# Sparse attention and a routed expert layer on one core: expert 0 run batch by batch among the next batch's attention, x transposed on TensorE, weights cast by their DMA, masks on VectorE

## The chip, the cores and the metric

One core of one Trainium2 chip. The metric is the device time of one execution in microseconds. Each experiment ran beside the kernel before on one chip, but different experiments ran on different chips, so two experiments are best compared by their ratios to the kernel before. "Span" is the length of the one profiled execution, about 1 to 2 us under the time.

The engines: TensorE (PE in the profile; PEld is its weight load, which overlaps: 788.8 and 389.4 us busy in the kernel before's span of 848.3 us), VectorE (DVE), ScalarE (ACT), GpSimd (POOL), SyncE (SP, which here only issues DMAs).

## The reference, cut to what matters

```python
# attention: q, k, v are (4 batches, 8 heads, 768 positions, 64)
k_sum = k.reshape(B, H, 24, 32, D).max(axis=3)      # 24 blocks of 32 keys
v_sum = v.reshape(B, H, 24, 32, D).mean(axis=3)
scores_l = scale * q @ k^T, kept where |i - j| < 16 # a band
scores_s = scale * q @ k_sum^T + log(32)            # 24 summary keys
a = softmax over both together;  x = a @ [v, v_sum] # -> x (3072, 512)

# routing: P = exp(x @ w_gate), 8 rounds of Sinkhorn: rows, columns, * N/E
# experts: for e in range(8):                       # dense: every row, every expert
#     out += P[:, e:e+1] * (relu(x @ w1[e]) @ w2[e])  # 512 -> 1024 -> 512
```

The routing weight multiplies an expert's result at the very end, so expert 0 can be computed before the routing is known, as soon as rows of x exist. Rows of x exist batch by batch, 768 rows each. Both kernels use this, to a very different degree.

The expert matmuls are the bulk of the work: 8 experts x 6 blocks of 512 rows x 64 matmuls (32 for the hidden layer, 32 for the projection) of 512 columns, 3072 in all.

## The kernel before: the parts that matter

Attention goes by pairs of heads (16 pairs, four to a batch). The mask is a multiplication on GpSimd. Results of a batch collect in `x_sb`; x then gets transposed by a way through DRAM ("the bridge").

```python
E_t = [attn.tile([128, G, EW], BF16, name=f"Et{i}") for i in range(NEB)]
for i in range(NEB):                                  # start-up, a row of memsets
    nc.gpsimd.memset(E_t[i][:, :, 0:EPL], 0.0)
    nc.gpsimd.memset(E_t[i][:, :, EPL + WIN:], 0.0)
    ...
    nc.gpsimd.memset(E_sum[i][:, :], 0.0)
...
def head_mask(i, j):
    nc.gpsimd.tensor_tensor(out=et[...], in0=et[...], in1=band[...], op=ALU.mult)
...
def store_batch(b):
    nc.sync.dma_start(out=x_dram[b * 768:(b + 1) * 768, :]..., in_=x_sb[b % NXB][:])
def xbar_batch(b):
    for g in range(KD):
        nc.sync.dma_start_transpose(out=xT[:, g, b * 768:(b + 1) * 768],
                                    in_=x_dram[b * 768:(b + 1) * 768, g * 128:(g + 1) * 128])
```

Of expert 0 only the hidden layer of its first two 512-row blocks is put among the attention of pairs 7 to 15, in halves of 256 columns (`mm1_drip`):

```python
            if i == 7 and PREFILL >= 1:
                drip += [(0, 0, f) for f in range(2 * KF)]
            if i == 10 and PREFILL >= 2:
                drip += [(0, 1, f) for f in range(2 * KF)]
```

The expert stage: the hidden layer has two PSUM buffers (`fpsum`), the projection four. Weights are loaded as fp32 by SyncE into one staging tile and cast by VectorE or ScalarE.

```python
fpsum = ctx.enter_context(tc.tile_pool(name="fpsum", bufs=2, space=...PSUM))
ypsum = ctx.enter_context(tc.tile_pool(name="ypsum", bufs=4, space=...PSUM))
def mm1(e, n, fpool, eng2):                           # hidden layer
    for f in range(KF):
        hp = fpool.tile([128, 512], FP32, tag="h", name="hps")
        for dk in range(KD):
            nc.tensor.matmul(hp[:], lhsT=w1x[e % 2][...], rhs=xT[:, dk, n * 512:(n + 1) * 512], ...)
        # relu out of PSUM: f even on ScalarE, f odd on VectorE
```

The softmax here doesn't subtract the row's maximum and nothing guards it: scores larger than these inputs give would overflow.

Of the kernel before, what the change touches and what calls it, by code (L numbers as in the profile page):

```python
# [13 lines left out]
AX = mybir.AxisListType  # L14


@with_exitstack
def kernel(
# [20 lines left out]
    NG = N // 512  # L39
    SCALE = 1.0 / float(D) ** 0.5  # L40
    WIN = 192
    LIVE = 158
    EPL = 112
    EW = EPL + WIN + 80
    NPAIR = (B * H) // 2

    PREFILL = 2
# [3 lines left out]
    dram = ctx.enter_context(tc.tile_pool(name="dram", bufs=1, space=bass.MemoryType.DRAM))  # L51
    fpsum = ctx.enter_context(tc.tile_pool(name="fpsum", bufs=2, space=bass.MemoryType.PSUM))
# [4 lines left out]
    band = const.tile([128, WIN], BF16)  # L57
    nc.gpsimd.memset(band, 1.0)
    nc.gpsimd.affine_select(out=band, in_=band, compare_op=ALU.is_ge, fill=0.0,
                            base=-1, pattern=[[1, WIN]], channel_multiplier=-1)  # L60
    nc.gpsimd.affine_select(out=band, in_=band, compare_op=ALU.is_ge, fill=0.0,
                            base=31, pattern=[[-1, WIN]], channel_multiplier=1)

    MBW = 148
    m_big = const.tile([128, MBW], BF16)
    nc.gpsimd.memset(m_big, 1.0)
    nc.gpsimd.affine_select(out=m_big, in_=m_big, compare_op=ALU.is_ge, fill=0.0,
                            base=640, pattern=[[-32, MBW]], channel_multiplier=1)
    nc.gpsimd.affine_select(out=m_big, in_=m_big, compare_op=ALU.is_ge, fill=0.0,
                            base=-609, pattern=[[32, MBW]], channel_multiplier=-1)  # L70

# [16 lines left out]
    wst = [persist.tile([128, 4096], FP32, name=f"wst{i}") for i in range(1)]  # L88
    w1_a = persist.tile([128, KD * F], BF16)
    w2_a = persist.tile([128, KF * DM], BF16)  # L90
    hT_sb = [persist.tile([128, KF, 512], BF16, name=f"hT{i}") for i in range(2)]
    nc.gpsimd.memset(crec_sb, 0.0)

    x_dram = dram.tile([N, DM], BF16, name="x_bridge")

    nc.scalar.dma_start(out=wg_f32[:], in_=moe_w_gate.rearrange("(dk p) e -> p dk e", p=128))
    nc.gpsimd.tensor_copy(out=wg_bf[:], in_=wg_f32[:])

    def load_w1(e, st, part=None):
        src = moe_w1[e].rearrange("(dk p) f -> p dk f", p=128)  # L100
        if part is None:
            nc.sync.dma_start(out=wst[st][:], in_=src)
        else:
            nc.sync.dma_start(out=wst[st][:].rearrange("p (dk f) -> p dk f", dk=KD)[:, part, :],
                              in_=src[:, part, :])

    def load_w2(e, st, part=None):
        src = moe_w2[e].rearrange("(fk p) d -> p fk d", p=128)
        if part is None:
            nc.sync.dma_start(out=wst[st][:], in_=src)  # L110
        else:
            nc.sync.dma_start(out=wst[st][:].rearrange("p (fk d) -> p fk d", fk=KF)[:, 2 * part:2 * part + 2, :],
                              in_=src[:, 2 * part:2 * part + 2, :])

    def cast_w(st, dst, eng):
        if eng is nc.scalar:
            nc.scalar.copy(out=dst[:], in_=wst[st][:])  # L117
        else:
            eng.tensor_copy(out=dst[:], in_=wst[st][:])

    w1x = [w1_a, None]
    w2x = [w2_a, None]
    hfill = [None]

    def mm1(e, n, fpool, eng2):
        for f in range(KF):
            hp = fpool.tile([128, 512], FP32, tag="h", name="hps")
            for dk in range(KD):
                nc.tensor.matmul(  # L129
                    hp[:],  # L130
                    lhsT=w1x[e % 2][:, dk * F + f * 128:dk * F + (f + 1) * 128],
                    rhs=xT[:, dk, n * 512:(n + 1) * 512],
                    start=(dk == 0), stop=(dk == KD - 1))
            if f % 2 == 0:
                nc.scalar.activation(out=hT_sb[n % 2][:, f, :], in_=hp[:],  # L135
                                     func=AF.Relu, bias=0.0, scale=1.0)
            else:
                eng2.tensor_scalar_max(out=hT_sb[n % 2][:, f, :], in0=hp[:],  # L138
                                       scalar1=0.0)

    def mm1_drip(e, n, fpool, f):
        hp = hfill[0]
        if f % 2 == 0:
            hp = fpool.tile([128, 512], FP32, tag="h", name="hps")
            hfill[0] = hp
        half = f % 2
        fr = f // 2
        for dk in range(KD):
            nc.tensor.matmul(  # L149
                hp[:, half * 256:half * 256 + 256],  # L150
                lhsT=w1x[e % 2][:, dk * F + fr * 128:dk * F + (fr + 1) * 128],
                rhs=xT[:, dk, n * 512 + half * 256:n * 512 + half * 256 + 256],
                start=(dk == 0), stop=(dk == KD - 1))
        if half == 0:
            nc.scalar.activation(out=hT_sb[n % 2][:, fr, 0:256], in_=hp[:, 0:256],
                                 func=AF.Relu, bias=0.0, scale=1.0)
        else:
            nc.vector.tensor_scalar_max(out=hT_sb[n % 2][:, fr, 256:512],  # L158
                                        in0=hp[:, 256:512], scalar1=0.0)

    with tc.tile_pool(name="attn", bufs=1) as attn, \
         tc.tile_pool(name="pw", bufs=1, space=bass.MemoryType.PSUM) as pw, \
         tc.tile_pool(name="avp", bufs=1, space=bass.MemoryType.PSUM) as avp:

        NQKB = 2
        NVB = 2
        NTRB = 3
        NEB = 4
        NVE = 3
        NXB = 2  # L170

        qq_st = [attn.tile([128, G, 128], FP32, name=f"qqst{i}") for i in range(NQKB)]
        kk_st = [attn.tile([128, G, 128], FP32, name=f"kkst{i}") for i in range(NQKB)]
        vv_f32 = [attn.tile([128, G, 2, 65], FP32, name=f"vvf{i}") for i in range(NVB)]
        qq_bf = [attn.tile([128, G, 128], BF16, name=f"qqb{i}") for i in range(2)]
        kk_bf = [attn.tile([128, G, 128], BF16, name=f"kkb{i}") for i in range(2)]
        vv_ext = [attn.tile([128, G, 2, 65], BF16, name=f"vve{i}") for i in range(NVE)]
        qqT = [attn.tile([128, 16 + S + 48], BF16, name=f"qqT{i}") for i in range(NTRB)]
        kkT = [attn.tile([128, S], BF16, name=f"kkT{i}") for i in range(NTRB)]
        ksumT = [attn.tile([128, 128], BF16, name=f"ksumT{i}") for i in range(NTRB)]  # L180
        E_t = [attn.tile([128, G, EW], BF16, name=f"Et{i}") for i in range(NEB)]
        E_sum = [attn.tile([128, S], BF16, name=f"Esum{i}") for i in range(NEB)]
        vsum_ext = [attn.tile([128, 65], BF16, name=f"vsum{i}") for i in range(NEB)]
        recip = [attn.tile([128, G, 1], FP32, name=f"recip{i}") for i in range(NEB)]
        x_sb = [attn.tile([128, G, DM], BF16, name=f"xsb{i}") for i in range(NXB)]

        for i in range(NVB):
            nc.gpsimd.memset(vv_f32[i][:, :, :, 64:65], 1.0)
        for i in range(NTRB):
            nc.gpsimd.memset(qqT[i][:, 0:16], 0.0)  # L190
            nc.gpsimd.memset(qqT[i][:, 16 + S:], 0.0)
            nc.gpsimd.memset(ksumT[i][:, 24:128], 0.0)
        for i in range(NEB):
            nc.gpsimd.memset(E_t[i][:, :, 0:EPL], 0.0)
            nc.gpsimd.memset(E_t[i][:, :, EPL + WIN:], 0.0)
            nc.gpsimd.memset(E_t[i][:, :, EPL:EPL + 1], 0.0)
            nc.gpsimd.memset(E_t[i][:, :, EPL + 1 + LIVE:EPL + WIN], 0.0)
            nc.gpsimd.memset(E_sum[i][:, :], 0.0)
            nc.gpsimd.memset(vsum_ext[i][:, :], 0.0)
            nc.gpsimd.memset(vsum_ext[i][0:24, 64:65], 32.0)  # L200

        def ptile(shape, dtype, tag, name):
            return pw.tile(shape, dtype, tag="work", name=name, bufs=5)

        def load_pair(i, eng=None, split=False):
            b = i // 4
            h0 = (i % 4) * 2
            eng = eng or nc.sync
            eng2 = nc.scalar if split else eng
            for j in range(2):  # L210
                eng.dma_start(
                    out=qq_st[i % NQKB][:, :, j * 64:(j + 1) * 64],
                    in_=q[b, h0 + j].rearrange("(g p) d -> p g d", p=128))
                eng2.dma_start(
                    out=kk_st[i % NQKB][:, :, j * 64:(j + 1) * 64],
                    in_=k[b, h0 + j].rearrange("(g p) d -> p g d", p=128))
            for j in range(2):
# [130 lines left out]
        for i in range(NPAIR):  # L348
# [3 lines left out]
            if i + 2 < NPAIR:  # L352
                load_pair(i + 2)
# [178 lines left out]
```

## Time and profile before

| | before |
|---|---|
| time, median of 3 runs | 845.96 us (841.19 to 850.69) |
| span of the profiled run | 848.3 us |
| first TensorE instruction of attention | 14.12 us |
| last values matmul of attention | 176.7 us |
| x of the last batch is all back (its routing matmuls wait for the last piece) | 187.5 us |
| one hidden layer of 512 rows, 32 matmuls | 7.14 to 7.15 us |
| one projection of 512 rows, 32 matmuls | 6.91 us |

The page's row of TensorE's busy tenths and of its granted clock, each digit a fortieth of the span (21 us):

```profile
PE   2886787689999999999999999999999999999998
...
PEclk9955599579999999999999999999999999999999
```

The first eight or nine slices are attention: TensorE is partly idle, and the throttle grants it half its clock in a good part of them. After that it is over 90% busy at full clock. This trace has whole stretches of 20 us at 0.50 (80 to 100 us) and at 1.00 (200 us and later), and some with a mean between; what makes the throttle grant one or the other is not shown. A busy digit at half clock is worth half of one at full clock: the 22 values matmuls of a head take 0.68 us at full clock and 1.38 us at half.

The same stage by stretches of 20 us (columns: stretch and length, then busy time and instructions of PE, PEld, DVE, ACT, POOL, then the clock, the DMA share and GB/s):

```profile
80.00:100.00 20.00, 14.69 (x141) 10.34 (x139) 10.30 (x14) 10.16 (x30) 10.27 (x4) 0.50 0.70 170
...
160.00:180.00 20.00, 13.27 (x157) 9.85 (x159) 6.76 (x16) 4.70 (x14) 4.10 (x3) 0.50 0.12 43
```

No engine is full here. The start of the trace (columns: start, duration, engine, line, operation, output and input; in brackets the idle time before it and what ended it):

```profile
5.29 0.66 POOL L194 MEMSET Et_134<- 128x672 bf16 x1
5.48 8.58 DVE L226 CAST qqb_118<-qqst_112 128x768 bf16<-128x768 f32 x1 [4.13 <-DMA qqst_112<-in_q_dram]
...
13.46 0.19 POOL L199 MEMSET vsum_145<- 128x65 bf16 x1
13.98 0.54 DVE L227 CAST kkb_120<-kkst_114 128x768 bf16<-128x768 f32 x1
14.12 0.82 PE L235 MATMUL tq<-ident,qqb_118 128*128 128x128 bf16 x6 [14.12 <-DVE qqb_118 L226]
```

The cast of q takes 8.58 us and the cast of k, of the same shape, 0.54 us. The first one starts inside GpSimd's row of memsets and ends 0.4 us after that row (13.65 us).

The end of attention in the chain of waits (start, duration, what):

```profile
177.60 3.68 DMA x_bridge<-xsb_151
...
181.30 1.14 SPq L327
...
182.49 1.27 SPq L327
...
183.82 3.63 DMA xT<-x_bridge
```

That is the bridge: 10 us from the last x to its transposed copy. The timeline of TensorE in the same 10 us:

```profile
178.46 7.35 PE L451 MATMUL yps<-w_a,hT_97 128*128 128x512 bf16 x27 [0.22 <-issue]
...
185.67 0.81 PE L451 MATMUL yps<-w_a,hT_97 128*128 128x512 bf16 x3
```

These are projections of expert 0 for blocks whose hidden layer had been done inside attention. And the expert stage in the chain of waits:

```profile
401.27 5.35 PE hps L129 x24
...
406.65 0.70 DVE hT_98 L138
...
407.39 1.02 PE hps L129 x4
408.42 6.91 PE yps L451 x32
```

A hidden layer lasts 7.15 us (401.27 to 408.42), the projection with the same number of matmuls 6.91 us. In the hidden layer the chain runs through a 0.70 us eviction on VectorE: the last group had to wait for a PSUM buffer.

### The profile page before, as it was taken

The numbers are of one execution on the slowest core, as the hardware profiler recorded it, in microseconds if no ns is written. First come the engines' busy times: TensorE is split into PE (matmuls) and PEld (weight loads), VectorE is DVE, ScalarE is ACT, GpSimd is POOL, SyncE is SP. The second block draws the span as 40 slices with busy tenths as digits, with TensorE's granted clock in tenths as the row PEclk, the third lists the DMA queues.
The fourth block names the chain that finished last, engine by engine and source line by source line (L and its number), as shares of the span: only waits on it lengthen the run. The fifth ranks groups of instructions, "written<-read, shape, count | busy, mean of one in ns | idle before, by whom it ended". The sixth has DMA issues, their size and how long they took to land.

```text
span 848.3 us, 11203 instructions
## 1 busy us (share of the span) xinstructions
PE 788.8 (93%) x4546; PEld 389.4 (46%) x4608; DVE 402.4 (47%) x623; ACT 221.1 (26%) x434; POOL 77.8 (9%) x85
## 2 busy tenths in 40 slices
PE   2886787689999999999999999999999999999998
PEld 2665565544444444444444444444444444444443
DVE  6754576447655444444454444444544544444443
ACT  2644356523131212221311113113111131111110
POOL 6542334210000000000000000000000000000000
PEclk9955599579999999999999999999999999999999
DMA  9978688544022003200320022002200200001122
GB/s 177 174 179 197 159 186 190 159 114 160 1 100 100 0 1 100 100 1 0 100 100 1 0 100 100 1 0 100 100 1 0 100 1 1 0 1 50 51 99 100
DMA packets 107876, 65.76 MB, mean 78 GB/s; under 512 B 89392, under 2 KB 92464, under 8 KB 107824
## 3 DMA queue, kind: packets, MB, share of 16 engines
q1 hardware_dynamic: 104944, 64.43, 27.3%
q10 hardware_dynamic: 2880, 0.61, 0.5%
q8 instruction: 36, 0.59, 0.3%
q14 instruction: 16, 0.13, 0.1%
HBM read 52.45 MB, written 9.44 MB: 73 GB/s over the span
## 4 chain that ended last, share of the span: by engine, by line
PE 85%; DVE 6%; ACT 3%; issue 2%; DMA 2%; POOL 0%; SPq 0%; ACTq 0%; DVEq 0%; POOLq 0%
PE hps L129 37%; PE yps L451 37%; PE av L310 4%; PE hps L149 2%; PE ss L266 2%; PE sg L255 1%; PE tq L235 1%; PE tk L237 1%; DMA vvf_116<-in_v_dram 1%; PE vs L288 1%; DVE kkb_120 L227 1%; DVE xsb_151 L314 1%; POOL Et_134 L278 0%; DVE ksumT_131 L242 0%; DMA x_bridge<-xsb_151 0%
## 5 line engine op out<-in xcount | busy, mean ns | idle before, releaser
L462 DVE SCALAR_TENSOR_TENSOR out_acc<-yps,P_sb,out_acc 128x512 f32<-128x512 f32 x168 | 125.8, 751 | 153.5 <-PE yps L451 148.0
L129 PE MATMUL hps<-xT,w_b 128*128 128x512 bf16 x753 | 174.8, 378 | 1.6 <-ACT hT_97 L135 0.4
L129 PE MATMUL hps<-xT,w_a 128*128 128x512 bf16 x689 | 161.6, 378 | 1.2 <-DVE hT_98 L138 0.2
L135 ACT ACTIVATE hT_97<-hps 128x512 bf16<-128x512 f32 x92 | 54.9, 597 | 255.4 <-PE hps L129 243.5
L129 PEld LDWEIGHTS <-w_b 128*128 128x128 bf16 x768 | 74.4, 97 | 97.5 <-issue 17.7
L451 PEld LDWEIGHTS <-hT_97 128*128 128x128 bf16 x768 | 75.2, 99 | 91.6 <-issue 2.4
L135 ACT ACTIVATE hT_98<-hps 128x512 bf16<-128x512 f32 x92 | 54.6, 597 | 240.1 <-PE hps L129 232.0
L451 PEld LDWEIGHTS <-hT_98 128*128 128x128 bf16 x768 | 74.9, 98 | 89.1
L138 DVE TENSOR_SCALAR hT_97<-hps 128x512 bf16<-128x512 f32 x92 | 63.6, 692 | 95.7 <-PE hps L129 95.7
L138 DVE TENSOR_SCALAR hT_98<-hps 128x512 bf16<-128x512 f32 x92 | 63.6, 691 | 95.3 <-PE hps L129 95.3
L129 PEld LDWEIGHTS <-w_a 128*128 128x128 bf16 x704 | 67.8, 97 | 88.4 <-issue 16.4
L451 PE MATMUL yps<-w_a,hT_97 128*128 128x512 bf16 x376 | 87.6, 384 | 1.5 <-DVE xsb_151 L314 0.9
L451 PE MATMUL yps<-w_a,hT_98 128*128 128x512 bf16 x376 | 85.2, 379 | 0.5 <-issue 0.2
L451 PE MATMUL yps<-w_b,hT_97 128*128 128x512 bf16 x375 | 84.5, 379 | 0.4
L451 PE MATMUL yps<-w_b,hT_98 128*128 128x512 bf16 x377 | 84.5, 379 | 0.4
L149 PE MATMUL hps<-xT,w_a 128*128 128x256 bf16 x128 | 21.4, 297 | 0.5 <-DVE hT_98 L158 0.5
L278 POOL TENSOR_TENSOR Et_134<-Et_134,band 128x948 bf16<-128x948 bf16 x8 | 17.9, 2240 | 35.3 <-ACT Et_134 L260 35.3
L117 ACT CAST w_b<-wst_94 128x4096 bf16<-128x4096 f32 x4 | 14.4, 3605 | 25.3 <-PE yps L451 21.6
L278 POOL TENSOR_TENSOR Et_136<-Et_136,band 128x948 bf16<-128x948 bf16 x8 | 15.9, 1984 | 50.1 <-ACT Et_136 L260 50.1
L226 DVE CAST qqb_118<-qqst_112 128x768 bf16<-128x768 f32 x8 | 17.5, 2181 | 4.1 <-DMA qqst_112<-in_q_dram 4.1
L235 PE MATMUL tq<-ident,qqb_118 128*128 128x128 bf16 x48 | 5.8, 275 | 14.1 <-DVE qqb_118 L226 14.1
L278 POOL TENSOR_TENSOR Et_137<-Et_137,band 128x948 bf16<-128x948 bf16 x8 | 16.3, 2040 | 6.0 <-ACT Et_137 L260 5.9
(181 smaller groups left out, 575.3 us busy)
## 6 DMA issues: line engine op xcount, KB each, us to landing
wst_94<-in_moe_w_dram SPq DMA_DIRECT2D x14, 2048.0 KB, 8.2
out_dram<-out_acc SPq DMA_DIRECT2D x24, 256.0 KB, 2.0
wst_94<-in_moe_w_dram SPq DMA_DIRECT2D x8, 512.0 KB, 5.2
qqst_112<-in_q_dram SPq DMA_DIRECT2D x16, 192.0 KB, 3.6
qqst_113<-in_q_dram SPq DMA_DIRECT2D x16, 192.0 KB, 3.9
kkst_115<-in_k_dram SPq DMA_DIRECT2D x16, 192.0 KB, 4.1
vvf_117<-in_v_dram SPq DMA_DIRECT2D x16, 192.0 KB, 4.3
vvf_116<-in_v_dram SPq DMA_DIRECT2D x15, 192.0 KB, 4.1
```

The source lines that it names most:

```text
L117: nc.scalar.copy(out=dst[:], in_=wst[st][:])
L129: nc.tensor.matmul(hp[:], lhsT=w1x[e % 2][:, dk * F + f * 128:dk * F + (f + 1) * 128], rhs=xT[:, dk, n * 512:(n + 1) * 512], start=(dk == ...
L135: nc.scalar.activation(out=hT_sb[n % 2][:, f, :], in_=hp[:], func=AF.Relu, bias=0.0, scale=1.0)
L138: eng2.tensor_scalar_max(out=hT_sb[n % 2][:, f, :], in0=hp[:], scalar1=0.0)
L149: nc.tensor.matmul(hp[:, half * 256:half * 256 + 256], lhsT=w1x[e % 2][:, dk * F + fr * 128:dk * F + (fr + 1) * 128], rhs=xT[:, dk, n * 51 ...
L226: nc.vector.tensor_copy(out=qq_bf[i % 2][:], in_=qq_st[i % NQKB][:])
L235: nc.tensor.transpose(tqv[:, g, :], qq_bf[i % 2][:, g, :], ident)
L266: nc.tensor.matmul(ss[:, :], lhsT=ksumT[i % NTRB][p0:p0 + 64, :], rhs=qtile[p0:p0 + 64, 16 + half * 384:16 + (half + 1) * 384], start=True ...
L278: nc.gpsimd.tensor_tensor(out=et[:, :, EPL + 1:EPL + 1 + LIVE], in0=et[:, :, EPL + 1:EPL + 1 + LIVE], in1=band[:, None, 1:1 + LIVE].to_bro ...
L310: nc.tensor.matmul(av[:, c, :], lhsT=lhsT, rhs=rhs, start=(mi == 0), stop=(mi == len(mms) - 1))
L451: nc.tensor.matmul(yp[:], lhsT=hT_sb[n % 2][:, f, t4 * 128:(t4 + 1) * 128], rhs=w2x[e % 2][:, f * DM:(f + 1) * DM], start=(f == 0), stop=( ...
L462: nc.vector.scalar_tensor_tensor(out=out_acc[:, t, :], in0=yp[:], scalar=psl, in1=out_acc[:, t, :], op0=ALU.mult, op1=ALU.add)
```

## The change

The intent: fill TensorE's idle time in attention with expert 0, all of it, batch by batch; drop the bridge; drop the staging casts; give the hidden layer more PSUM buffers. The core of the diff (the rest renames, or packs scores and summary values of two heads into fewer instructions):

```diff
-def head_mask(i, j):
-    nc.gpsimd.tensor_tensor(out=et[...], in0=et[...], in1=band[...], op=ALU.mult)
+    nc.vector.tensor_tensor(out=et, in0=et, in1=band[...], op=ALU.mult)   # in scores(i)

-def store_batch(b): ...      # x to DRAM
-def xbar_batch(b): ...       # transposing load back
+def to_xT(i, xs):            # one pair's x, 6 transposes on TensorE
+    tx = aps.tile([128, S], BF16, tag="a", name="tx")
+    for g in range(G):
+        nc.tensor.transpose(tx[:, g * 128:(g + 1) * 128], xs[:, g, :, :]..., ident)
+    nc.scalar.copy(out=xT[:, dk, b * S:(b + 1) * S], in_=tx[:])

-def load_w1/load_w2 (fp32 by SyncE into staging), cast_w (VectorE or ScalarE)
+def load_w(e, gate=None):    # the DMA casts fp32 to bf16
+    if gate is not None:     # a one-element write makes the load wait for `gate`
+        nc.gpsimd.tensor_copy(out=w1[0:1, 0, 0:1], in_=gate)
+        nc.gpsimd.tensor_copy(out=w2[0:1, 0, 0:1], in_=gate)
+    nc.gpsimd.dma_start(out=w1[:], in_=moe_w1[e]...)
+    nc.gpsimd.dma_start(out=w2[:], in_=moe_w2[e]...)

+for i in range(NP):          # 16 pairs
+    load(i + 2)
+    if i == 1: load_w(0, kst[3][0:1, 0, 0, 0:1])
+    scores(i);  drip(2)
+    transposed(i + 1);  drip(1)
+    vsum(i)
+    if i > 0:
+        to_xT(i - 1, xs)
+        if i % 4 == 0:       # a batch is complete
+            logits(b)
+            fill += first_expert(two halves of 384 rows)   # 8 hidden + 3 projection each
+            if b == 0: load_w(1)
+    drip(1);  xs = values(i);  drip(2)
...
-fpsum 2 buffers for the hidden layer, ypsum 4 for the projection
+mps2 4 buffers for the hidden layer, mps 3 for the projection
```

The last batch of expert 0 runs after attention, with Sinkhorn's steps strewn in between.

## The prediction

> **What bounds it now.** Two stages. Attention lasts until about 177 us, then comes a bubble until 187 us: the chain of waits shows 177.6 to 187.5 us going to the store of x to DRAM and the transposing load back. From 187 us the experts run, and by the busy time per 100 us TensorE is then 99% busy at clock 1.0. The page's "PE 85% of the chain" is mostly this stage.
>
> In attention TensorE isn't the limit. At full clock the 22 values matmuls of a head take 0.68 us, in the half-clock stretches (40 to 100 and 140 to 180 us) 1.39 us. I estimate 3.7 us of TensorE work per head pair, while a pair takes about 10 us: it waits on the chain score, exp (ACT), mask (GpSimd, 1.98 us a head), values.
>
> In the expert stage an (expert, 512 tokens) step takes 14.06 us. The projection's 32 matmuls take 6.91 us (216 ns each[...]); the hidden layer's take 7.15 us. With two PSUM buffers the next group waits for an eviction (0.69 us on DVE plus its latencies, against 0.86 us of matmuls).
>
> **What the change does.**
> 1. Three of four batches of expert 0 (hidden and projection, about 62 us of TensorE) move into attention's idle TensorE time, where before only 64 matmuls' worth were. TensorE per pair becomes 3.7 + 5.6 = 9.3 us. DVE per pair: casts 1.65,[...] reduce 0.95, qT 0.66, x scaling 1.5, sums 0.4, plus 1.6 of expert evictions: about 8.5 us. So pairs 4 to 15 run at about 10.3 us, nearly today's pace, but with expert 0 inside.
> 2. The bridge disappears: about 10 us.
> 3. Four and three PSUM buffers remove the hidden layer's stall: 0.24 us x 42 = 10 us.
> 4. Weights are cast by the DMA: 28.8 us of ACT and 18 us of DVE casts vanish, all off the critical path.
>
> **A loss.** The instruction order shows six hidden matmuls of expert 0 hoisted into pair 3's scores. TensorE runs in order, so it stops there (about 37 us) until w1 of expert 0 lands. GpSimd's queue waits for pair 3's k (about 25 us) and then issues expert 1's w1 *before* expert 0's: 4 MB must pass, sharing the engines with the q, k, v loads (about 200 GB/s in all in the DMA row). I expect it at 50 to 65 us: a stall of about 18 us.
>
> **Sum.** First matmul 13 us; pairs 0 to 2 at 7.5 us, 36 us; stall to 55; rest of pair 3 and pair 4, 69; eleven pairs, 182; leftover 187; last batch's expert 0 (21 us) with sinkhorn and logits, 211; 2688 matmuls at 216 ns = 581, 792; start-up slips, half-clock pairs, tail: about 802.
>
> **Right or wrong.** The chain should have no x bridge; the hidden layer's 32 matmuls take 6.91 us; TensorE is over 90% busy from pair 4 on at clock 1.0; one gap before a w1 matmul at 37 to 55 us; expert 1 starts about 210 us; pairs with filler take 10 to 11 us.
>
> **What would make it wrong.** Casting DMAs much slower than 200 GB/s (longer stall, over 830). DVE bounding the filled pairs at 12 to 13 us (+25 us): masks or casts dearer than estimated. Sinkhorn's DVE chain, now squeezed into 21 us of matmuls, stopping TensorE by over 5 us. Or a smaller stall (785).
>
> Predicted 802 us, range 778 to 828; faster by over 2%: 0.91, within 2%: 0.07, slower: 0.02.

The six other terms of VectorE are estimates from the kernel before's trace (such as 0.55 us for each of three casts, 0.95 us for the reduce, 0.42 to 0.69 us for an expert's eviction) and come to 6.8 us; the author's "about 8.5 us" holds the cut one, too. The pace of 10.3 us a pair was set above TensorE's 9.3 us. The 3.7 us in that is the author's estimate, and rests on the 0.68 us of a head's values and on the timeline of the kernel before at full clock (108 to 125 us, clock 1.00). "TensorE runs in order" was said without a trace; the changed kernel's shows it (under "The stall" below).

## The result, and the profile after

| | before | after |
|---|---|---|
| time, median of 4 runs each | 844.48 us (841.19 to 850.69) | 778.03 us (777.42 to 778.59) |
| ratio | | 0.9208 (95%: 0.917 to 0.9247) |
| span | 848.3 us | 776.6 us |
| first TensorE instruction of attention | 14.12 us | 5.39 us |
| last values matmul | 176.7 us | 160.7 us |
| x of the last batch is all back (in the new kernel, its first routing matmul) | 187.5 us | 166.1 us |
| hidden layer, 32 matmuls of 512 columns | 7.14 to 7.15 us | 6.91 us |
| expert 1 starts | | 191.5 us |

A ratio is the mean time of one kernel's runs over the mean of the other's runs of the same rounds, so it isn't quite the ratio of the medians beside it.

The change is 8% faster. All outputs are right. The time lies at the very edge of the predicted range, 24 us under the central value of 802 us.

The page's rows of TensorE:

```profile
PE   5649999999999999999999999999999999999997
...
PEclk9769999999999999999999999999999999999999
```

Besides the last slice, only the first three are left in which TensorE isn't full. By stretches of 20 us, with the columns as before:

```profile
40.00:60.00 20.00, 10.81 (x140) 8.43 (x141) 10.84 (x26) 5.41 (x9) 0.00 (x0) 0.66 1.05 214
80.00:100.00 20.00, 19.89 (x266) 12.62 (x266) 17.28 (x42) 11.54 (x23) 0.00 (x0) 1.00 0.79 179
140.00:160.00 20.00, 19.71 (x256) 12.93 (x255) 14.03 (x33) 10.70 (x21) 0.00 (x0) 1.00 0.01 2
```

From 60 us to 160 us the stage is bounded by TensorE itself, at full clock, with VectorE at 14 to 18 of 20 us. The one bad stretch is 20 to 60 us, where the DMA share is full (1.05 to 1.14) and the mean clock 0.66 to 0.75. The start, in the timeline:

```profile
4.74 0.60 DVE L199 CAST kb<-kst 128x768 bf16<-128x768 f32 x1 [0.68 <-DMA kst<-in_k_dram]
5.39 0.82 PE L203 MATMUL tk<-ident,kb 128*128 128x128 bf16 x6 [5.39 <-DVE kb L199]
6.37 1.03 POOL L174 MEMSET E_115<- 128x678 bf16 x1
7.61 0.80 DVE L193 CAST vx_121<-vst 128x768 bf16<-128x768 f32 x1 [0.85 <-DMA vst<-in_v_dram]
```

The cast takes 0.60 us in place of 8.58 us: in the new program GpSimd has other work first (mask constants), so its long memsets start at 6.37 us, after the casts of k and q have started (4.74 and 6.12 us). Here it is memsets that stretch: three of the eight take 1.03 to 1.08 us, the others 0.66 to 0.71. The stretch between attention and the last batch, where the bridge was, in TensorE's timeline:

```profile
160.77 3.40 PE L128 MATMUL yps<-w_322,h 128*128 128x512 bf16 x15
...
166.07 0.74 PE L347 MATMUL sink<-wg_bf,xT 128*128 128x8 bf16 x24
166.67 2.60 PE L116 MATMUL hps<-xT,w_321 128*128 128x384 bf16 x15
```

Left-over projections of the batch before cover the last transposes. The expert stage in the chain of waits:

```profile
406.37 4.96 PE hps L116 x23
...
411.38 1.89 PE hps L116 x8
413.27 6.91 PE yps L128 x32
```

No eviction is on the chain any more; the hidden layer takes 6.91 us, too (406.37 to 413.27, rounded in the lines). And the bad stretch. TensorE and VectorE in the timeline, then SyncE's queue, then GpSimd's issue of weights:

```profile
44.81 0.56 DVE L199 CAST kb<-kst 128x768 bf16<-128x768 f32 x1 [8.12 <-DMA kst<-in_k_dram]
45.43 0.82 PE L203 MATMUL tk<-ident,kb 128*128 128x128 bf16 x6 [7.68 <-DVE kb L199]
49.57 0.82 PE L207 MATMUL tq<-ident,qb 128*128 128x128 bf16 x6 [2.04 <-DVE qb L200]
```

```profile
14.42 1.30 SPq L187 DMA_DIRECT2D kst<-in_k_dram  x2
...
20.11 8.50 SPq L187 DMA_DIRECT2D kst<-in_k_dram  x2
28.65 10.64 SPq L187 DMA_DIRECT2D qst<-in_q_dram  x2
39.39 7.63 SPq L191 DMA_DIRECT2D vst<-in_v_dram  x2
```

```profile
18.21 0.89 POOL L109 DMA_DIRECT2D w_810<-in_moe_w_dram  x1
19.10 0.75 POOL L109 DMA_DIRECT2D w_321<-in_moe_w_dram  x1
...
20.71 1.05 POOL L110 DMA_DIRECT2D w_811<-in_moe_w_dram  x1
```

All four weight loads (w1 and w2 of experts 0 and 1, 2 MB of fp32 each) are issued within 3 us, expert 1's w1 (`w_810`) first. From then on an issue of two loads of pair 4's k takes SyncE 8.50 us in place of 1.30 us. TensorE stands still for 7.68 us for pair 4's k, not for weights: expert 0's w1 (`w_321`) took 15.4 us from issue to landing, so it was there at 34.5 us, before its first matmul at 36.4 us.

An account of the 71.7 us between the two spans, cut at the same event in both, the return of the last batch's x. A full-speed expert matmul of 512 columns is 6.91 us / 32 = 0.216 us:

| | before | after | gain |
|---|---|---|---|
| until the first TensorE instruction | 14.1 | 5.4 | 8.7 |
| from there to the return of the last batch's x, less the expert matmuls inside at full speed | 150.3 | 98.5 | 51.8 |
| from there to the end, less the expert matmuls at full speed | 20.5 | 9.3 | 11.2 |

(Before: 187.5 - 14.1 = 173.4 us hold 128 matmuls of 256 columns and 43 of 512, worth 23.1 us. After: 166.1 - 5.4 = 160.7 us hold 192 of 384 columns and 144 of 512, worth 62.2 us. All 3072 together are worth 663.4 us.)

The account sets one execution against one, and that of the kernel before is from the slow end of its times: the medians differ by 66.4 us, not 71.7. Its attention scatters most. In the run with a third PSUM buffer below, which has the same attention code, the last values matmul ends at 168 us and not 176.7. So up to 9 us of the 51.8 us may be scatter.

### The profile page after: what moved, and what is told of

The parts are those of the page before. It is cut to its first block, busy times and chain, and to the rows that moved or that the text cites. A ratio compares the mean times of both kernels' runs of the same rounds, so it can differ in the third digit from the quotient of the medians. Undisturbed runs are those within 1.5% of the kernel's fastest.

```text
span 776.6 us, 10681 instructions
## 1 busy us (share of the span) xinstructions
PE 739.9 (95%) x4545; PEld 368.4 (47%) x4608; DVE 389.8 (50%) x703; ACT 185.3 (24%) x326; POOL 25.5 (3%) x50
## 4 chain that ended last, share of the span: by engine, by line
PE 88%; DVE 4%; SPq 3%; DMA 2%; ACT 1%; issue 1%; ACTq 0%; DVEq 0%
PE yps L128 41%; PE hps L116 40%; PE av L272 3%; SPq L187 2%; DMA qst<-in_q_dram 2%; PE sg L223 1%; PE tq L207 1%; PE vs L249 1%; PE tx L284 0%; DMA vst<-in_v_dram 0%; SPq L191 0%; PE ss L232 0%; DVE ksT_113 L211 0%; DVE h L123 0%; DVE csum_sb L359 0%
## 5 line engine op out<-in xcount | busy, mean ns | idle before, releaser
L128 PEld LDWEIGHTS <-h 128*128 128x128 bf16 x1536 | 149.2, 98 | 177.8 <-DVE h L123 0.3
L120 ACT ACTIVATE h<-hps 128x512 bf16<-128x512 f32 (+1 forms) x200 | 116.2, 581 | 488.0 <-PE hps L116 479.8
L123 DVE TENSOR_SCALAR h<-hps 128x512 bf16<-128x512 f32 (+1 forms) x200 | 133.7, 669 | 164.7 <-PE hps L116 163.1
L116 PE MATMUL hps<-xT,w_321 128*128 128x384 bf16 x256 | 50.8, 330 | 0.0
L128 PE MATMUL yps<-w_322,h 128*128 128x512 bf16 x183 | 43.3, 379 | 0.5 <-issue 0.2
L116 PE MATMUL hps<-xT,w_810 128*128 128x512 bf16 x188 | 42.4, 379 | 0.2
L116 PE MATMUL hps<-xT,w_3081 128*128 128x512 bf16 x189 | 42.3, 379 | 0.2
L128 PE MATMUL yps<-w_4182,h 128*128 128x512 bf16 x189 | 42.3, 379 | 0.2
L116 PE MATMUL hps<-xT,w_5257 128*128 128x512 bf16 x188 | 42.2, 379 | 0.3
L116 PE MATMUL hps<-xT,w_4719 128*128 128x512 bf16 x189 | 42.3, 379 | 0.2
L128 PE MATMUL yps<-w_4720,h 128*128 128x512 bf16 x188 | 42.2, 379 | 0.2
L116 PE MATMUL hps<-xT,w_5795 128*128 128x512 bf16 x188 | 42.2, 379 | 0.2
L128 PE MATMUL yps<-w_3082,h 128*128 128x512 bf16 x188 | 42.2, 379 | 0.2
L128 PE MATMUL yps<-w_3644,h 128*128 128x512 bf16 x188 | 42.2, 379 | 0.2
L116 PE MATMUL hps<-xT,w_3643 128*128 128x512 bf16 x187 | 42.2, 379 | 0.3
L128 PE MATMUL yps<-w_5796,h 128*128 128x512 bf16 x189 | 42.1, 379 | 0.2
L116 PE MATMUL hps<-xT,w_4181 128*128 128x512 bf16 x188 | 42.0, 379 | 0.2
L128 PE MATMUL yps<-w_811,h 128*128 128x512 bf16 x188 | 42.0, 379 | 0.2
L128 PE MATMUL yps<-w_5258,h 128*128 128x512 bf16 x187 | 42.0, 379 | 0.2
L116 PEld LDWEIGHTS <-w_5795 128*128 128x128 bf16 x192 | 18.8, 98 | 22.6
L116 PEld LDWEIGHTS <-w_3643 128*128 128x128 bf16 x192 | 18.8, 98 | 22.6
## 6 DMA issues: line engine op xcount, KB each, us to landing
w_321<-in_moe_w_dram POOLq DMA_DIRECT2D x1, 1024.0 KB, 15.4
```

The lines of the kernel that those rows point to most:

```text
L116: nc.tensor.matmul(hp[:, 0:n], lhsT=w1s[e][:, dk, f * 128:(f + 1) * 128], rhs=xT[:, dk, t0:t0 + n], start=(dk == 0), stop=(dk == KD - 1))
L120: nc.scalar.activation(out=h[:, f, 0:n], in_=hp[:, 0:n], func=AF.Relu, bias=0.0, scale=1.0)
L123: nc.vector.tensor_scalar_max(out=h[:, f, 0:n], in0=hp[:, 0:n], scalar1=0.0)
L128: nc.tensor.matmul(yp[:], lhsT=h[:, f, c * 128:(c + 1) * 128], rhs=w2s[e][:, f, :], start=(f == 0), stop=(f == KF - 1))
```

## The experiments

The theory, formed on the two traces: (A) most of the gain is expert 0 in idle TensorE time; the hidden layer's third and fourth PSUM buffers are worth about 10 us; the early start is worth 6 to 9 us, and it comes from the casts no longer lying beside GpSimd's memsets; masks and weight casts are worth nothing by themselves; and the gap at 40 us comes from the weight queue starving the q, k, v loads. The rivals are named run by run.

### No expert work inside attention

The changed kernel with expert 0 run whole after attention.

```diff
                     logits(b)
-                    for half in range(2):
-                        fill += list(first_expert(b * S + half * HS, HS, mps))
 ...
-b = B - 1
-for half in range(2): for step in first_expert(b * S + half * HS, HS, mps2): ...
+for b in range(B):
+    for half in range(2): for step in first_expert(b * S + half * HS, HS, mps2): ...
```

> The new kernel, but expert 0 of all four batches runs after attention instead of among it. Theory A (the interleave is the main gain: 62 us of expert 0 run in time in which TensorE would otherwise idle): attention without filler keeps the 8.0 us per pair that pairs 1 and 2 show, so it ends about 140 to 147 us instead of 161, and 62 us of experts come after it: about 815 us, +38 over the new kernel's 778. Rival B (attention itself became that much faster, and the filler only stretches it): at most +15, below 793.

Measured: 819.32 us (815.77 to 820.41), ratio to before 0.9675. That is 41 us above the changed kernel. The last values matmul ends at 140 us in place of 160.7 us, and the last batch's x is all back at 142.5 us in place of 166.1 us. So 62 us of expert matmuls before it cost 23.6 us there; the other 39 us ran in time that is idle without them. Theory A holds for the filler. These 39 us are the filler's worth against no filler at all; the kernel before hid a part of its own 23.1 us already.

### The old attention alone, first try

```diff
-    PREFILL = 2
+    PREFILL = 0
```

> The kernel before without its 64 matmuls' worth of expert 0 among attention, to set attention alone beside attention alone (141 us until the last values matmul in the new kernel without filler, 177 us here with its small filler). Theory (the old attention is bound by its own chain of score, exp, mask, values and not by TensorE): attention ends at 172 to 178 us all the same, and the 14 us of matmuls come after it: 855 to 862. Rival (the small filler was what stretched it): attention ends at 160 us or less and the time stays at 844 to 848.

Measured: 850.21 us (847.09 to 852.95), ratio 1.0041 (0.9991 to 1.0092): no difference can be told. The run doesn't answer its question. In its trace 64 hidden matmuls of expert 0 (72 by their weight loads, as some records are missing) still run between 92 and 140 us: they were moved there from the expert stage, as it seems by the scheduler, which found w1 and x ready. A source edit that stops asking for work does not keep a scheduler from doing it; a dependence does.

### The old attention alone, by a dependence

Here the cast of expert 0's w1 first reads a value of the last pair's x, so no hidden matmul can come earlier.

```diff
-    PREFILL = 2
+    PREFILL = 0
-            if i == 7:
-                cast_w(0, w1_a, nc.vector)
         ...
         xbar_batch(B - 1)
+        nc.vector.tensor_copy(out=w1_a[0:1, 0:1], in_=x_sb[(B - 1) % NXB][0:1, G - 1, DM - 1:DM])
+        cast_w(0, w1_a, nc.vector)
     # load and cast of w2 of expert 0 after attention, too
```

> The kernel before with nothing of expert 0 inside attention, this time by data: the cast of expert 0's w1 reads a value of the last pair's x first, so no hidden matmul can be hoisted (the earlier try without filler failed for that). Read: when the last values matmul ends. What the question is: how much of the gain of the attention stage is the new attention itself, and how much is better use of its idle TensorE time. Theory M (most of the 36 us between the two attention stages is filler used better): the old attention alone ends at 150 to 160 us, 10 to 20 us over the new attention alone (141 us). Rival N (the old chain score, exp, mask on GpSimd, values sets the pace, filler or not): it still ends at 168 us or later, and the new attention alone is over 27 us shorter. The whole time is expected at 850 to 875 us (w2 of expert 0 is loaded and cast later too), and no verdict rests on it.

Measured: 862.64 us (861.72 to 866.38), ratio 1.0222. The last values matmuls of this run, and then those of the new attention alone (the run without filler above), in TensorE's timeline:

```profile
169.65 0.25 PE L310 MATMUL av<-vsum,Esum 128*128 128x65 bf16 x1
169.71 0.30 PE L310 MATMUL av<-vve,Et 128*128 128x65 bf16 x2
173.39 10.97 PE L129 MATMUL hps<-xT,w_a 128*128 128x512 bf16 x39 [3.39 <-DVE w_a L119]
```

```profile
139.84 0.19 PE L272 MATMUL av<-vsx,Es 128*128 128x65 bf16 x1
139.87 0.23 PE L272 MATMUL av<-vx,E 128*128 128x65 bf16 x2
```

The old attention alone ends at 170 us. What I expected of theory M, 150 to 160 us, is refuted, and rival N's numbers hold: the old attention is slow without filler, too. From the first TensorE instruction (14.4 and 5.4 us) it lasts 155.6 us, the new one 134.7 us. So of the 51.8 us in the account, about 21 us are a shorter attention, by one execution each. The other 31 us hold three things that these runs don't separate: more of expert 0 in idle time, a shorter way from the last values to the return of x (10.8 us before, 2.4 us in the run without filler), and the scatter named above. So the filler need not be most of the gain over the kernel before, as theory A has it. Which part of the rewritten attention (masks, fewer and larger instructions for scores and summary values, the transposes) makes the 21 us was not taken apart. Nor was the clock: its mean is 0.66 in these 155.6 us and 0.81 in the 134.7 us, so a part of the 21 us may be TensorE's speed and not the shape of the code.

### Two PSUM buffers for the hidden layer in the changed kernel

```diff
-    mps2 = ...(name="mps2", bufs=4, space=PSUM)
+    mps2 = ...(name="mps2", bufs=2, space=PSUM)
```

> The new kernel with two PSUM buffers for the hidden layer after attention instead of four. Theory (the second bank's eviction held TensorE 0.24 us in each step of 64 matmuls): 32 hidden matmuls take 7.15 us again, 42 steps, +10 us: 788. Rival (the steady stage got faster for another cause, as the weight casts that are gone): no change, 778.

Measured: 791.06 us (790.01 to 791.64), ratio 0.9347: 13 us slower than with four. A hidden layer takes 7.20 us in its chain of waits, the projection stays at 6.91 us; 42 hidden layers in experts 1 to 7 make 42 x 0.29 = 12 us.

```profile
411.89 7.20 PE hps L116 x32
```

### A third PSUM buffer in the kernel before

```diff
+            hpool = xpool[0] if f % 3 == 2 else fpool
-            hp = fpool.tile([128, 512], FP32, tag="h", name="hps")
+            hp = hpool.tile([128, 512], FP32, tag="h", name="hps")
-    ypsum bufs=4
+    ypsum bufs=3, and a pool of one buffer as xpool[0]
```

> The kernel before, with a third PSUM bank for the hidden layer after attention (and three instead of four for the projection). Theory: the same stall as in the run with two banks, seen from the other side: 32 hidden matmuls take 6.91 us instead of 7.15, 46 such groups, about -11 us: 834. Rival (in the kernel before something else, such as the weight casts on ACT and VectorE, holds the steady stage): less than -3 us.

Measured: 836.89 us (828.82 to 839.33), ratio 0.9868 (0.9801 to 0.9936): 9 us faster by the medians, which is under the 2% that count as faster but clear of the noise (5 to 17 us by the interval). Its hidden layers take 6.91 us. From both sides the buffers are worth 9 to 13 us. One buffer more is enough.

### GpSimd's memsets on VectorE in the kernel before

```diff
-            nc.gpsimd.memset(E_t[i][:, :, 0:EPL], 0.0)      # and the three others of E_t
-            nc.gpsimd.memset(E_sum[i][:, :], 0.0)
+            nc.vector.memset(E_t[i][:, :, 0:EPL], 0.0)
+            nc.vector.memset(E_sum[i][:, :], 0.0)
```

> The kernel before with the zeroing of its eight attention buffers on VectorE, which idles until 5 us, instead of GpSimd. Theory (the first q cast took 8.58 us on VectorE because GpSimd's row of memsets kept it out): that cast takes 0.6 us, the first matmul starts at 6 to 7 us instead of 14.1, and attention and all that follows moves up by 6 to 8 us: about 838. Rival (the first cast waited for data): the first matmul starts within 1.5 us of before and the time stays within 2 us.

Measured: 840.27 us (836.17 to 840.94), ratio 0.9911 (0.9854 to 0.9969): 6 us faster by the medians, again under 2% but clear of the noise.

```profile
10.86 0.82 PE L235 MATMUL tq<-ident,qqb 128*128 128x128 bf16 x6 [10.86 <-DVE qqb L226]
```

The first matmul comes at 10.86 us in place of 14.12, and no cast at the start takes over 0.57 us (it would have come earlier still, had the scheduler not put the v cast first, which waited for its load until 9.77 us). So the 8.58 us was the memsets beside the cast. The expected first matmul at 6 to 7 us is missed. The start-up's 3.3 us lie within the gain's interval, 3 to 12 us; whether they count to the end in full is not shown.

### Expert 1's weights later

```diff
                 if i == 1:
                     load_w(0, kst[3][0:1, 0, 0, 0:1])
+                if i == 6:
+                    load_w(1, kst[8][0:1, 0, 0, 0:1])
 ...
-                    if b == 0:
-                        load_w(1)
```

> The new kernel, but expert 1's weights are loaded only after pair 8's k has landed, so that 4 MB less run against the q, k, v loads between 18 and 48 us. Theory C (TensorE's gap of 37.7 to 45.4 us is the k of pair 4, starved by the weight queue): the gap shrinks by about the 14 us that those 4 MB take, TensorE's other waits take some back: 766 to 770. Rival D (the gap is the wait for expert 0's w1, as I predicted): w1 of expert 0 comes first in its queue now and lands 8 us earlier, but pair 4's k is as late as before only if it was never the cause; then the gap would end at the landing of w1 and not at that of k. Rival E (the attention stage is bound elsewhere and later pairs give it back): 776 to 779.

Measured: 770.09 us (768.54 to 770.36), ratio 0.9096: 8 us faster than the changed kernel. Pair 4's k transposes in its timeline, to be read against the 45.43 us line above:

```profile
35.97 0.51 PE L203 MATMUL tk<-ident,kb 128*128 128x128 bf16 x6 [0.68 <-DVE kb L199]
```

The wait falls from 7.68 to 0.68 us. Nothing but 4 MB of expert 1's loads was moved, so the gap came with them.

### Every early weight load gated by itself

```diff
-                if i == 1:
-                    load_w(0, kst[3][0:1, 0, 0, 0:1])
+                # w1 of expert 0 waits for kst[3], its w2 for kst[5],
+                # w1 and w2 of expert 1 for kst[15]
-                    if b == 0:
-                        load_w(1)
```

> The new kernel with all early weight loads spread behind the q, k, v loads: w1 of expert 0 after pair 3's k, its w2 after pair 5's, expert 1 after pair 15's. With the run that moved expert 1 alone (770 us) the same theory: every 2 MB that run against the q, k, v loads cost TensorE waits. Expected: the wait of 2.6 us at 31 us and those at 65 to 80 us of that run go, 762 to 766. Rival (the pairs without filler are bound by their own chain at 8 us, and weights no longer matter): 769 to 770, as the earlier run.

Measured: 769.15 us (768.54 to 769.24), ratio 0.9068. The expected 762 to 766 us is missed; it is no better than the simpler gate. A likely reason stands in its timeline, and the next run tests it:

```profile
6.70 0.67 POOL L180 MEMSET E<- 128x678 bf16 x1
7.19 4.83 DVE L199 CAST vx<-vst 128x768 bf16<-128x768 f32 x1 [0.79 <-DMA vst<-in_v_dram]
...
12.62 0.58 PE L229 MATMUL sg<-qT,kT 64*128 64x158 bf16 x6 [5.34 <-DVE vsx L183]
```

The cast of v took 4.83 us beside GpSimd's memsets, where the changed kernel had got away with 0.80 us, and the first scores came at 12.62 us in place of 9.01 us. The instructions stand in the same order in both. What the traces show to differ is under half a microsecond: v's cast starts at 7.19 us in place of 7.61, the memsets at 6.70 in place of 6.37. That this decides it was not tested.

### The same, with the memsets on VectorE: the fastest kernel

```diff
         for t in E_t:
-            nc.gpsimd.memset(t[:, :, 0:EPL], 0.0)
-            nc.gpsimd.memset(t[:, :, EPL + LIVE:], 0.0)
+            nc.vector.memset(t[:, :, 0:EPL], 0.0)
+            nc.vector.memset(t[:, :, EPL + LIVE:], 0.0)
```

> The changed kernel with the weight loads gated one by one as in the last such run (769.2 us), and the memsets of the E buffers on VectorE in place of GpSimd. In that run the first v cast took 4.83 us beside GpSimd's row of memsets, and the first scores came 3.6 us later than in the changed kernel. Theory: with no long memsets on GpSimd the first v cast takes under 1 us, the first scores come at about 9 us, and the time is 765 to 766 us. Rival: the start is not on the path to the end (the loads' queue sets the pace of pairs 0 to 3 whenever they start), and it stays at 768.5 to 770 us.

Measured: 764.91 us (763.85 to 767.21), ratio 0.9055 (0.9004 to 0.9106), about as the theory had it. In its timeline:

```profile
7.84 0.54 DVE L199 CAST vx<-vst 128x768 bf16<-128x768 f32 x1
9.70 0.58 PE L229 MATMUL sg<-qT,kT 64*128 64x158 bf16 x6 [0.74 <-DVE vsx L183]
```

The v cast takes 0.54 us, the first scores come 2.9 us earlier than in the run above, and the median falls by 4.2 us. The size of that is open: the runs are from different chips, the ratios overlap, and the two profiled executions differ by 2.0 us. The memsets, 0.62 us each on VectorE, cost a little in turn: the first k cast waits behind them until 6.90 us. This version beats both kernels, by 13 us the changed one, and there the intervals of the ratios don't overlap.

### The bridge back, for the last batch alone

```diff
+        if i // PB == B - 1: xs = x_sb[:, :, i % PB, :, :]   # collect the last batch's x
-        to_xT(NP - 1, xs)
+        bridge(B - 1)         # store to DRAM, four transposing loads back
```

> The new kernel, but the last batch's x goes to DRAM and comes back through the transposing load as before, instead of TensorE transposes. Prediction on record: the bridge is worth about 10 us. Theory: store 3.7 us, transposing load about 6 us, of which the 5 us of filler left at that point hide about half: +5 to +7 us, 783 to 785; TensorE then has a gap of 5 to 6 us before the logits of the last batch. Rival (TensorE idles for the whole bridge): +10 us.

Measured: 782.29 us (780.86 to 783.32), ratio 0.9239 (0.9198 to 0.928): 4.3 us slower by the medians, though the interval overlaps that of the changed kernel. TensorE waits 2.84 us and then 0.35 us for the transposing loads; left-over projections cover the rest. The v cast at this run's start was held up, too (4.60 us), but its last values matmul ended at 159.1 us, no later than the changed kernel's. So what the trace shows of the bridge is 3.2 us of waits. The prediction had put it at about 10 us.

### Masks on GpSimd in the changed kernel

```diff
-                    nc.vector.tensor_tensor(out=et, in0=et,
+                    nc.gpsimd.tensor_tensor(out=et, in0=et,
```

> The new kernel with the four masks of a pair back on GpSimd. Theory (the filled pairs are bound by TensorE at 9.0 us, the mask is hidden by filler matmuls; only pairs 0 to 3 see the longer chain, about 1.5 us each, and the DVE casts now wait for GpSimd's masks): +5 to +10 us, 783 to 788. Rival (mask on VectorE is a main part of the gain, since GpSimd takes 1.98 us a head and values wait for it): over +20 us, above 798.

Measured: 779.13 us (778.34 to 779.93), ratio 0.9207 (0.9173 to 0.9241): the same as the changed kernel's 0.9208. My expectation of 5 to 10 us is refuted. That casts on VectorE can wait for GpSimd's masks is seen in the kernel before: two casts that began beside a mask of 1.98 and 2.17 us, at 40.48 and 42.87 us, took 2.15 and 2.02 us in place of 0.55. A mask's wait is hidden: of TensorE's waits in this run only one is for a mask, 1.2 us.

### Weights cast by engines again

```diff
-        if n == 1 and e + 1 < E:
-            load_w(e + 1)
+        if e + 1 < E:
+            stage_w(e + 1, n)   # fp32 by SyncE, cast on ScalarE or VectorE, experts 2 to 7
```

> The new kernel, but the weights of experts 2 to 7 are loaded as float32 and cast on ACT (3.6 us each) and VectorE (2.3 us each), as before. Theory on record (these casts were off the critical path): within 2 us of 778. Rival (a cast holds back the evictions behind it in its engine's queue, and TensorE runs out of PSUM banks): 12 casts, 1 us each or more, above 786.

Measured: 777.0 us (776.36 to 777.62), ratio 0.9162 (0.9121 to 0.9204): no loss. In the changed kernel, with its four buffers, these casts are off the critical path, so dropping them gains nothing, as predicted. That they cost nothing in the kernel before, with its two buffers, was not tested.

## Why the prediction was wrong by 24 us, point by point

The direction and the mechanism were right; the sum was too high. The terms of the sum, in the prediction's own steps:

| step of the sum | predicted | measured | difference |
|---|---|---|---|
| first matmul | 13 | 5.4 | -7.6 |
| pairs 0 to 2 | 23 (to 36) | 27.9 (to 33.3) | +4.9 |
| stall, pairs 3 and 4 | 33 (to 69) | 28.1 (to 61.4) | -4.9 |
| eleven filled pairs | 113 (to 182) | 99.3 (to 160.7) | -13.7 |
| leftover | 5 (to 187) | 6.0 (to 166.7) | +1.0 |
| the last batch of expert 0 | 24 (to 211) | 24.8 (to 191.5) | +0.8 |
| 2688 matmuls to the end | 581 | 585.1 (to 776.6) | +4.1 |
| "start-up slips, half-clock pairs, tail" | 10 | in the rows above | -10 |

(The cuts lie at a pair's last values matmul, to 0.2 us.)

**The step that failed: "So pairs 4 to 15 run at about 10.3 us, nearly today's pace".** They ran at 99.3 / 11 = 9.0 us. The two sums under it were a little high: TensorE 9.3 us a pair (98.1 us busy over eleven pairs is 8.9) and VectorE 8.5 us (81.5 us is 7.4). What was wrong is mostly the microsecond put on top of TensorE's sum. The prediction doesn't say what for; it reads as an allowance for the two engines waiting on each other. TensorE is 98.1 of 99.3 us busy there, at full clock, so such waits are almost gone once filler stands in its queue. The run with masks on GpSimd says the same from the other side: a head's mask took 1.98 us on GpSimd in the kernel before and takes two steps of 0.41 us on VectorE in the changed one, yet in that run TensorE waits for a mask only once, for 1.2 us. The run without filler shows where the old picture of "waits on the chain" came from: without filler TensorE is busy 57.7 us of the 78.5 us from 61.4 to 139.9 us, at a mean clock of 0.83. The two stretches, the changed kernel first (columns as before):

```profile
61.40:160.70 99.30, 98.13 (x1263) 63.93 (x1267) 81.53 (x195) 55.62 (x106) 0.00 (x0) 1.00 0.47 105
...
61.40:139.90 78.50, 57.74 (x938) 46.51 (x938) 62.73 (x157) 39.46 (x73) 0.00 (x0) 0.83 0.55 124
```

**"First matmul 13 us" stayed near the old trace's 14.1 us without asking what made it so late.** One line at the start, a cast of 8.58 us beside one of the same shape that took 0.54 us, would have told. The traces show that a VectorE cast can be held up: 0.54 us alone, 8.58 us beside a row of 27 GpSimd memsets and 4.83 us beside eight, each of which is under 0.8 us. Two runs without those memsets on GpSimd show it gone (no first cast over 0.57 us). What holds the cast, no run here shows.

**The stall was right in time and place, and wrong in its cause and size.** Predicted: TensorE stops for about 18 us until expert 0's w1 lands at 50 to 65 us, as weights and q, k, v share the engines. Measured: w1 landed at 34.5 us, and TensorE stopped for 7.68 and 2.04 us, 9.7 us in all, for pair 4's k and q. The sharing was the error. From 20 to 48 us the weights' queue moved 4.18 MB as written, the q, k, v queue 1.24 MB. The weights read twice what they write, so the four of them (8.4 MB) were read in 30 us, 18.2 to 47.9 us: about 280 GB/s, against 44 GB/s for q, k, v, whose loads went in packets of 250 bytes (4957 for the 1.24 MB). That the size of packets is the reason was not tested. Expert 0's w1 took 15.4 us from issue to landing, the w1 loads of the expert stage 7.9 to 8.6 us. That TensorE keeps its order shows in the same stretch: expert 0's next four hidden matmuls, with w1 there since 34.5 us and the last write to x's transposed copy done at 31.6 us, ran only at 46.05 us, behind the k transposes. The run with expert 1's weights moved out of the way took the gap away, and its 8 us. In the run with masks on GpSimd the order is another one and TensorE does wait 7.1 us for a weight; both causes lie close together, and both come with weight loads issued early.

**The bridge as "about 10 us" was a wrong reading of the chain.** The chain of waits showed that the last batch's x came 10 us after its values, not that TensorE was idle. In the old trace projections ran through it (the 7.35 us line); in the new kernel, putting it back for the last batch shows 3.2 us of waits.

**PSUM buffers: right.** Predicted 10 us; the account's last row, which holds this and the tail, says 11.2 us, and the two runs 13 and 9 us. A matmul of 512 columns at clock 1.00, with a weight load before each, takes 6.91 us / 32 = 216 ns in both kernels' projections and now in the hidden layers, too. That gave the 2688 matmuls' 581 us, right within 4 us.

**Casts off the path: right** in the changed kernel (the run with engine casts: 777.0 us). **Masks on VectorE** (the estimate is cut): 0.41 us each, four a pair, 1.64 us. **"Sinkhorn's DVE chain" squeezed into 21 us of matmuls stopping TensorE by over 5 us:** it did not; the last batch took 24.8 us with it, 0.8 us over the sum. Pairs 0 to 2 took 27.9 us and not 23 us: the first alone took 12.1 us from the first matmul to its last values, and why was not tested.

**The slack of 10 us was counted twice.** Half-clock pairs and slips are already in a pace that is read from a trace. Where the pace is a sum of engine times, the slack belongs in the range, not in the central value.

## What to carry to other kernels

When an engine that is short of work gets independent filler in its queue, start from its own sum of busy time at full clock, and don't add the waits of the chain it had before: here the filler hid them (98.1 of 99.3 us busy at clock 1.00, against 57.7 of 78.5 us at 0.83 without filler). A gap on the chain of waits is a loss only if the engine's own timeline is empty there. Before reusing a start-up time or a stall from the old trace, find the one instruction that makes it; and gate early bulk loads, as four large loads issued at once starved the small ones that the next step waited for here (280 against 44 GB/s; with two of them later, the wait for pair 4's k fell from 7.68 to 0.68 us).
